# A small token block moved ahead at one turn of the work, and a batch's attention begun one stage earlier

## The chip, the cores and the metric

One core of a Trainium2 chip runs one program. The metric is the device time of one execution in microseconds (us). TensorE (PE) does the matmuls, VectorE (DVE), ScalarE (ACT) and GpSimd (POOL) the elementwise work, SyncE (SP) issues most transfers.

## What is computed

Three layers follow one another, all in float32:

```python
def _attn_ref(q, k, v):                       # 4 batches, 8 heads, 576 rows, 64 wide
    q_s = np.exp(q - q.max(-1)); q_s = q_s / (q_s.sum(-1) + 1e-09)
    k_s = np.exp(k - k.max(2));  k_s = k_s / (k_s.sum(2) + 1e-09)
    kv = np.einsum('bhsd,bhse->bhde', k_s, v)
    return np.einsum('bhsd,bhde->bhse', q_s, kv)

def _moe_ref(x, w_in, w_out):                 # 2304 tokens, 512 -> 2048 -> 512
    h = x @ w_in
    g = np.where(h >= 1, h, np.where(h <= -1, 0.0, (h + 1) ** 2 / 4))
    return g @ w_out

def _moe2_ref(x, domain_probs, w1, w2):       # 4 experts, 512 -> 1024 -> 512
    p = domain_probs / (domain_probs.sum(-1, keepdims=True) + 1e-09)
    for e in range(E):
        out += p[:, e:e + 1] * (np.maximum(x @ w1[e], 0.0) @ w2[e])
    return out
```

The second layer is called layer one below, the third the experts.

## The kernel before, in words

The 2304 tokens are five blocks: 0, 1, 2 and 4 of 512 tokens, 3 of 256. They are worked in two passes (`PASSES`): the first takes blocks 1 and 0 through layer one and then through all four experts, the second blocks 2 and 4 as a pair, with block 3 as its `rest`. Attention of batches 0 and 1 runs at the start of the program, that of batches 2 and 3 beside the first pass; each batch is four units, a unit being two heads.

A float32 product is made of three matmuls on split operands, a high and a low part of each (`products`, lines 1257 to 1261): the `x` tiles hold tokens, the `w` tiles weights, the `gate` tiles hidden values. The hidden layer's products ("ups") go into the PSUM tiles `bank` and `late_bank`; the products of the second matrix ("downs") go into `out_bank`. For a pair of blocks the ups are Strassen's seven products on quarter matrices (`strassen`, line 1449): sums of quarters of the tokens, called B11, T1, B21, T2, T3, T4 and B22, are made once per stage by `prepare` (line 1285), on DVE and POOL, and split into high and low by `split` (a cast on ACT or DVE, line 512 or 514, and a subtraction on DVE or POOL, line 517). Block 3's ups are plain products (`plain_rest`, line 1427). In the experts of the second pass the pair's downs are seven products too (`second_pairs`, line 1770), block 3's are plain (`group_downs`, line 1703).

The work is a list of groups of four chunks of hidden columns (`groups`). In the second pass each quarter or half of a weight matrix stands three times in the list, for blocks 2, 4, 3 in this order. The downs are issued in the order of this list. A group's ups can run ahead of its downs.

Nobody writes the order of instructions by hand. The program is built by a planner (`Order`): tasks are Python generators that ask for an engine and a duration, and of the tasks that can go on the planner takes the one with the earliest due step, with an allowance per kind of task. The order it finds is then fixed in each engine's queue. Steps count the chunks of the list, 0 to 239; the first pass's experts begin at step 32, the second pass at 96, its experts at 144.

What the change touches:

- Where layer one of the second pass ends and the experts begin ("the second turn"): the last downs of layer one are evicted into `acc` by `finish_first` (line 1888, DVE), `prepare` forms the seven sums out of `acc2` and `acc4` (blocks 2 and 4), and only then can the experts' first Strassen products run. Block 3's operand is split after all of the pair's operands are (`yield operands_in`).
- The same place of the first pass ("the first turn"), with blocks 1 and 0.
- Attention of batches 2 and 3: `load_units` (line 919) holds the first unit back until the event `calm`, which is set in `ups` when the second group of the first pass's experts begins, and the units' due steps are `to_experts + 10 + 5 * n`. A unit's PE instructions are transposes (lines 1108, 1112, 1206) and float32 matmuls (1138, 1216, two records for each), its DVE work is in lines 1105, 1110, 1171, 1190 and 517. When the last unit is done, `end_attention` gives its room to ten more gate tiles and one more PSUM bank to the ups.

Of the kernel before, what the change touches and what calls it, by code (L numbers as in the profile page):

```python
# [206 lines left out]
def attention_moe_kernel(  # L207
# [17 lines left out]
    KC = DM // P  # L225
# [37 lines left out]
    GATE_DUE = 1  # L263
    groups = []
    for pair, rest in PASSES:
        bs = [bi for bi in (*pair, rest) if bi is not None]
        for ws in (first, *experts):
# [5 lines left out]
            for i in range(0, len(ws), nj):  # L273
                groups += [(bi, ws[i:i + nj]) for bi in bs]
# [319 lines left out]
    part_in = {(ws[0], u): Event() for ws in jobs if len(ws) > 1 for u in range(4)}  # L594
    second_in = {(ws[0], u): Event() for ws in jobs if is_paired(ws[0]) for u in range(4)}
# [53 lines left out]
    def convert_weights():  # L649
        for ws in jobs:  # L650
# [20 lines left out]
            if is_paired(w):  # L671
# [6 lines left out]
                slot_of[w, 1] = us  # L678
                order.add(load_sums(w, 1, us[1:3], second_in), "load", due + 1)
# [593 lines left out]
    xop = {}  # L1273
    xop_in = {(i, kind, x, c): Event()
# [10 lines left out]
    def prepare(i, kind):  # L1285
# [63 lines left out]

        for k, x in enumerate(USE):  # L1350
            xop[i, kind, x] = ((yield xfree), (yield xfree))
            if not ts:
# [10 lines left out]
        if rest is not None:  # L1363
            xop[i, kind, "rest"] = ((yield xfree), (yield xfree))
            for c in range(KC):
                for event in come(rest, c):
                    yield event
            h, l = xop[i, kind, "rest"]
            yield operands_in[i, kind]
            t = yield from split(h, l, acc[rest], 1024)  # L1370
            rest_in[i, kind].set(t)
            used[rest].set(t)
# [9 lines left out]
    def ups():  # L1382
        for s, (g, j) in enumerate(steps):
# [3 lines left out]
            if w[0] == "b" or is_kept(w):  # L1387
                i, kind = w[3], w[0]
                pair, rest = PASSES[i]
                if bi == pair[0] and j % 2 == 0:  # L1390

                    ahead = 4 if kind == "a" and g == order_of[bi, kind][-1] else 0
# [8 lines left out]
                    if rest is not None:  # L1401
                        for k in range(2):
                            yield from plain_rest(i, g + 2, j + k)
# [4 lines left out]
            yield s  # L1408
            bank = yield ups_banks
# [13 lines left out]
            if s == last_a[bi]:  # L1423
                for x in xparts[bi]:
                    xfree.put(x, t)

# [22 lines left out]
    def strassen(i, g, j):  # L1449
# [7 lines left out]
        kind = w0[0]  # L1457
        at_end = j + 2 == len(ws) and g == order_of[bi, kind][-1]
# [512 lines left out]
```

## Time and profile before

| | |
|---|---|
| median of 3 runs | 1248.21 us (1247.08 to 1250.82) |
| the profiled execution | 1249.59 us |
| its span, first to last instruction | 1247.8 us |
| PE busy | 1221.9 us, 98% |
| DVE, POOL, ACT busy | 876.0, 683.9, 493.2 us |
| mean granted TensorE clock | 0.995 of full speed |

The engines' times overlap. A matmul's record is longer than its place in the queue: the next one starts before it ends, so the step from one start to the next is what a matmul costs PE, and idle time is what lies beyond the record's end.

### The profile page before, as it was taken

Reading aid. Unit: us, or ns where it says so; the run is one execution under the profiler, and the core shown is the slowest. Engines: PE = TensorE matmul, PEld = TensorE weight load, DVE = VectorE, ACT = ScalarE, POOL = GpSimd, SP = SyncE. Lnnn points to the kernel's source line nnn. Section 1 sums busy time; section 2 is a strip of 40 time slices with the busy share of each in tenths; the row PEclk is TensorE's granted clock in tenths of the full one; section 3 lists DMA queues with packets and bytes.
Section 4 is the critical chain, followed back from the end, with each engine's and each line's share of the span. In section 5 each row is a group of like instructions: output and inputs, shape, how many; then the busy total and the mean of one; then the engine's idle time right before and its main releaser. Section 6 shows DMA issues by size and latency. Waiting matters only on the chain.

```text
span 1247.8 us, 16455 instructions
## 1 busy us (share of the span) xinstructions
PE 1221.9 (98%) x5876; PEld 1007.1 (81%) x5876; DVE 876.0 (70%) x1318; ACT 493.2 (40%) x884; POOL 683.9 (55%) x595
## 2 busy tenths in 40 slices
PE   9999999999999999999999999999999999999996
PEld 8877778767787788888888888778888888888885
DVE  4866783699877877776733554578778777787786
ACT  4655654343443542232373354434223232232321
POOL 4453555444654565543785654343665675576653
PEclk9999999999999999999999999999999999999999
DMA  9863554225656453342553131504344244433313
GB/s 266 240 221 134 205 192 164 68 89 188 209 188 175 148 174 147 136 169 93 162 185 101 35 101 51 186 17 153 118 151 137 102 136 142 145 119 118 114 40 85
DMA packets 101170, 174.68 MB, mean 140 GB/s; under 512 B 25568, under 2 KB 59360, under 8 KB 101088
## 3 DMA queue, kind: packets, MB, share of 16 engines
q1 hardware_dynamic: 100288, 172.31, 42.1%
q10 hardware_dynamic: 800, 1.31, 0.4%
q8 instruction: 47, 0.77, 0.2%
q14 instruction: 35, 0.29, 0.1%
HBM read 118.53 MB, written 55.07 MB: 139 GB/s over the span
## 4 chain that ended last, share of the span: by engine, by line
PE 88%; DVE 7%; DMA 2%; ACT 1%; issue 1%; POOL 1%; SPq 0%; ACTq 0%; DVEq 0%; POOLq 0%
PE out_bank L1259 14%; PE out_bank L1260 14%; PE out_bank L1261 14%; PE bank L1259 7%; PE bank L1260 7%; PE bank L1261 7%; PE late_bank L1259 6%; PE late_bank L1260 6%; PE late_bank L1261 6%; PE bank L1254 2%; PE third L993 1%; DVE single L841 1%; PE late_bank L1138 1%; PE late_bank L1216 1%; DVE w L517 0%
## 5 line engine op out<-in xcount | busy, mean ns | idle before, releaser
L1259 PE MATMUL bank<-x,w 128*128 128x512 f32 (+1 forms) x490 | 185.5, 379 | 4.2 <-DVE cv L1689 2.2
L1260 PE MATMUL bank<-x,w 128*128 128x512 f32 (+1 forms) x490 | 182.5, 372 | 2.9 <-DVE x L517 2.7
L1261 PE MATMUL bank<-x,w 128*128 128x512 f32 (+1 forms) x490 | 182.0, 371 | 0.0
L517 POOL TENSOR_TENSOR w<-words,w 128x512 fp32r<-128x512 f32 (+2 forms) x87 | 116.9, 1355 | 110.7 <-ACT w L512 73.0
L1259 PE MATMUL late_bank<-x,w 128*128 128x512 f32 (+1 forms) x390 | 142.8, 366 | 1.4 <-POOL w L517 1.1
L1260 PE MATMUL late_bank<-x,w 128*128 128x512 f32 (+1 forms) x390 | 141.6, 363 | 0.0
L1261 PE MATMUL late_bank<-x,w 128*128 128x512 f32 (+1 forms) x390 | 141.4, 362 | 0.0
L1821 DVE TENSOR_TENSOR acc<-out_bank,acc 128x512 f32<-128x512 f32 x182 | 121.0, 687 | 24.9 <-PE out_bank L1261 24.6
L517 POOL TENSOR_TENSOR gate<-cv,gate 128x512 fp32r<-128x512 f32 (+1 forms) x59 | 76.1, 1298 | 93.2 <-ACT gate L512 91.8
L1259 PEld LDWEIGHTS bank<-x,w 128*128 128x128 f32 x490 | 92.4, 188 | 23.2 <-DVE cv L1689 3.0
L1260 PEld LDWEIGHTS bank<-x,w 128*128 128x128 f32 x490 | 92.5, 189 | 19.8 <-DVE x L517 4.3
L517 POOL TENSOR_TENSOR gate_late<-cv,gate_late 128x512 fp32r<-128x512 f32 (+1 forms) x57 | 72.1, 1272 | 60.6 <-ACT gate_late L512 60.3
L1261 PEld LDWEIGHTS bank<-x,w 128*128 128x128 f32 x490 | 92.3, 188 | 16.0
L1259 PE MATMUL out_bank<-w,gate 128*128 128x512 f32 x216 | 89.7, 415 | 0.3 <-DVE acc L1902 0.3
L1259 PE MATMUL out_bank<-gate,w 128*128 128x512 f32 (+1 forms) x224 | 85.5, 381 | 2.3 <-DVE acc L1888 2.3
L1259 PEld LDWEIGHTS late_bank<-x,w 128*128 128x128 f32 x390 | 73.7, 189 | 15.3 <-POOL w L517 1.5
L1260 PE MATMUL out_bank<-gate,w 128*128 128x512 f32 (+1 forms) x224 | 85.5, 382 | 0.0
L1261 PE MATMUL out_bank<-w,gate 128*128 128x512 f32 x216 | 85.4, 395 | 0.0
L1260 PE MATMUL out_bank<-w,gate 128*128 128x512 f32 x216 | 85.3, 395 | 0.0
L1261 PE MATMUL out_bank<-gate,w 128*128 128x512 f32 (+1 forms) x224 | 85.1, 380 | 0.0
L1260 PEld LDWEIGHTS late_bank<-x,w 128*128 128x128 f32 x390 | 73.8, 189 | 12.6 <-DVE x L517 0.4
L1261 PEld LDWEIGHTS late_bank<-x,w 128*128 128x128 f32 x390 | 73.8, 189 | 11.6
(320 smaller groups left out, 2919.4 us busy)
## 6 DMA issues: line engine op xcount, KB each, us to landing
words<-in_moe_w_dram SPq DMA_DIRECT2D x64, 512.0 KB, 4.5
sums<-w SPq DMA_DIRECT2D x64, 512.0 KB, 3.2
w<-sums SPq DMA_DIRECT2D x64, 512.0 KB, 4.3
kept<-w SPq DMA_DIRECT2D x32, 512.0 KB, 4.8
w<-kept SPq DMA_DIRECT2D x32, 512.0 KB, 4.9
words<-in_moe_w_in_dram SPq DMA_DIRECT2D x16, 512.0 KB, 3.8
words<-in_moe_w_out_dram SPq DMA_DIRECT2D x16, 512.0 KB, 5.2
wide<-in_q_dram SPq DMA_DIRECT2D x22, 160.0 KB, 3.2
```

What stands on the lines that cost most here:

```text
L517: (nc.vector if engine == DVE else nc.gpsimd).tensor_tensor(**kw)
L841: nc.vector.scalar_tensor_tensor(out=bits, in0=low, scalar=29, in1=bits, op0=ALU.logical_shift_right, op1=ALU.bitwise_or)
L993: nc.tensor.matmul(bank[:, :P].rearrange("p (h d) -> p h d", h=2), ek[:n, c], vt[:n, :, c], start=(c == 1), stop=(c == 0),)
L1138: nc.tensor.matmul(bank[:, :N], ek[:, c, :], vt_buf[:, c * N:(c + 1) * N], start=(c == 0), stop=(c == NC - 1),)
L1216: nc.tensor.matmul(bank[:, :hi - lo], bd, qt_buf[:, lo:hi], start=True, stop=True)
L1254: nc.tensor.matmul(bank[:, :P], ident, ident, start=True, stop=True)
L1259: nc.tensor.matmul(ps, al, bh, start=first, stop=False, **kw)
L1260: nc.tensor.matmul(ps, ah, bl, start=False, stop=False, **kw)
L1261: nc.tensor.matmul(ps, ah, bh, start=False, stop=last, **kw)
L1821: nc.vector.tensor_tensor(out=dst, in0=p, in1=dst, op=ALU.add)
```

## The change

The list of groups is altered at two places: the last quarter of layer one of the second pass goes in the order 2, 3, 4, and the first half of expert 0 in the order 3, 2, 4. At the first Strassen product of the experts, block 3's four plain products for that half are issued between the first and the second of the seven (`AT_TURN`). For them block 3's operand of the experts is split first and waits no longer for the pair's. The last Strassen group of layer one may start 6 steps ahead instead of 4 (`AHEAD_A`). The first weights of the second pass's experts are no longer held back until the pair's operands are there (`NO_WAIT`). Attention of batches 2 and 3 is due ten steps earlier, at the experts' first step, and is let go at step 28, under layer one of the first pass (`CALM`). The rest is bookkeeping for the planner (`xop_at`, `second_slots`, `beside`).

```diff
+    AT_TURN = 2
+    CALM = 28
+    LATE_AT = 0
+    LATE_BY = 5
+    NO_WAIT = 2
+    AHEAD_A = 6
...
-                groups += [(bi, ws[i:i + nj]) for bi in bs]
+                turned = bs
+                if rest is not None:
+                    if ws is first and i + nj == len(ws):
+                        turned = [pair[0], rest, pair[1]]
+                    elif ws is experts[0] and i == 0:
+                        turned = [rest, *pair]
+                groups += [(bi, ws[i:i + nj]) for bi in turned]
...
-        if step_of[w][0] > min(step_of[x][0] for x in chunks if (x[0], x[3]) == (w[0], w[3])):
+        if step_of[w][0] > min(step_of[x][0] for x in chunks if (x[0], x[3]) == (w[0], w[3])) + (NO_WAIT if w[0] == "b" and w[3] else 0):
             yield operands_in[w[3], w[0]]
...
-        att_due[b, hp] = s0 + LAG * hp if b < NOW else to_experts + 10 + 5 * ((b - NOW) * NP + hp)
+        att_due[b, hp] = s0 + LAG * hp if b < NOW else to_experts + LATE_AT + LATE_BY * ((b - NOW) * NP + hp)
...
+        if rest is not None and kind == "b":
+            xop[i, kind, "rest"] = ((yield xfree), (yield xfree))
+            order.add(rest_operand(i, kind, come, used), "ffn", due - 1)
...
-                    ahead = 4 if kind == "a" and g == order_of[bi, kind][-1] else 0
+                    ahead = AHEAD_A if kind == "a" and g == order_of[bi, kind][-1] else 0
...
-                    if g > order_of[0, "b"][0] and calm.time is None:
+                    if s >= CALM and calm.time is None:
                         calm.set(order.running.time)
...
-                    yield from strassen(i, g, j)
-                    if rest is not None:
-                        for k in range(2):
-                            yield from plain_rest(i, g + 2, j + k)
+                    of_rest = None if rest is None else beside(g, rest)
+                    turn = AT_TURN if rest is not None and of_rest < g else 0
+                    yield from strassen(i, g, j, 0 if j else turn)
+                    for k in ([j // 2] if not turn else [] if j else range(turn, len(ws) // 2)):
+                        if rest is not None:
+                            yield from rest_pair(i, of_rest, 2 * k)
...
+            if s == CALM and calm.time is None:
+                calm.set(order.running.time)
...
         if begins:
+            for k in range(turn):
+                yield from rest_pair(i, beside(g, PASSES[i][1]), 2 * k)
             p5 = yield from fifth()
```

**PE, the first turn.** The last downs of layer one and the experts' first products. `late_bank0` with `wide` or `ident` is attention's, `x12` and `x14` are T1 and B21, `x8` is T2. Before:

```order
L1261 MATMUL out_bank3_557<-gate2_1664,w2_94 128x512
L1259 MATMUL bank1_123<-x12_83,w5_97 128x512
...
L1259 MATMUL late_bank1_966<-x14_85,w4_96 128x512
...
L1261 MATMUL late_bank1_966<-x14_85,w4_96 128x512
L1259 MATMUL bank0_122<-x8_79,w5_97 128x512
```

After:

```order
L1275 MATMUL out_bank3_557<-gate2_1664,w2_94 128x512
L1230 MATMUL late_bank0_965<-wide0_136,kvbd00_141 128x256
L1273 MATMUL bank1_123<-x12_83,w5_97 128x512
...
L1230 MATMUL late_bank0_965<-wide0_136,kvbd00_141 128x320
...
L1273 MATMUL late_bank1_966<-x14_85,w4_96 128x512
...
L1152 MATMUL late_bank0_965<-wide4_140,wide3_139 128x130 x5
...
L1273 MATMUL bank0_122<-x8_79,w5_97 128x512
```

Three pieces of attention, of the first two units, now stand between the last down and the first product on T2; before, the first unit's matmuls came only after the turn.

**PE, the second turn.** `gate1` in the first piece is block 3's, `x2` is B11 and `x14` T1; in the second piece `gate2` is block 4's, `x14` is B11, `x2` block 3's operand, `x8` T1. Before:

```order
L1261 MATMUL out_bank3_557<-gate1_1663,w4_96 128x256
L1259 MATMUL bank0_122<-x2_73,w5_97 128x512
...
L1259 MATMUL late_bank0_965<-x14_85,w6_98 128x512
```

After:

```order
L1275 MATMUL out_bank3_557<-gate2_1664,w13_105 128x512
L1273 MATMUL late_bank0_965<-x14_85,w5_97 128x512
...
L1273 MATMUL bank0_122<-x2_73,w5_97 128x256
...
L1273 MATMUL out_bank0_554<-w3_95,gate_late8_3402 128x512
...
L1273 MATMUL bank1_123<-x8_79,w2_94 128x512
```

Before, the 48 matmuls of block 3's last downs (256 columns) stood between block 4's last down and the first product, and T1 came right behind it. Now block 4's downs come last, and between the first product and T1 stand block 3's four ups (12 matmuls of 256 columns each) and four products of its downs (12 matmuls of 512 columns).

**DVE, the second turn.** From the eviction of block 4's sums into `acc4` on. Before:

```order
L1888 TENSOR_TENSOR acc4_91<-out_bank3_557,acc4_91 128x512
L517 TENSOR_TENSOR acc2_89<-acc4_91,cv4_110 128x512
L517 TENSOR_TENSOR x15_86<-cv4_110,x14_85 128x512
L517 TENSOR_TENSOR x15_86<-cv3_109,x14_85 128x512
L517 TENSOR_TENSOR acc2_89<-acc4_91,cv3_109 128x512
L517 TENSOR_TENSOR x5_76<-acc2_89,x4_75 128x512
L1888 TENSOR_TENSOR acc3_90<-out_bank0_554,acc3_90 128x256
```

After:

```order
L1931 TENSOR_TENSOR acc4_91<-out_bank3_557,acc4_91 128x512
L529 TENSOR_TENSOR acc2_89<-acc4_91,cv4_110 128x512
L529 TENSOR_TENSOR x9_80<-cv4_110,x8_79 128x512
L529 TENSOR_TENSOR x9_80<-cv7_113,x8_79 128x512
L529 TENSOR_TENSOR acc2_89<-acc4_91,cv7_113 128x512
L1696 SCALAR_TENSOR_TENSOR gate_late8_3402<-bank0_122,gate_late8_3402 128x256
L1696 SCALAR_TENSOR_TENSOR gate_late9_3403<-bank1_123,gate_late9_3403 128x256
L529 TENSOR_TENSOR x11_82<-acc2_89,x10_81 128x512
```

Block 3's evictions into `acc3` and the split of its operand now stand ahead of block 4's evictions; in the chain of the pair's operands stand instead the four second halves of block 3's hidden values (line 1696).

## Rows read from the trace of the kernel before

**Rows 1.** PE's waits in the whole span: total us, times, longest.

```profile
PE bank L1260 <- DVE x L517: 2.7, 3, 1.6
PE out_bank L1259 <- DVE acc L1888: 2.3, 2, 1.9
```

**Rows 2.** Windows by stage; PEclk is the granted clock.

```profile
core 0: us, PE busy (x) PEld busy (x) DVE busy (x) ACT busy (x) POOL busy (x), PEclk, DMA share, GB/s
196.00:243.00 47.00, 47.00 (x206) 38.34 (x205) 20.50 (x28) 21.77 (x35) 29.83 (x26) 1.00 0.36 123
243.00:262.00 19.00, 17.14 (x68) 12.00 (x67) 17.21 (x26) 8.87 (x17) 6.17 (x4) 1.00 0.00 1
262.00:300.00 38.00, 36.91 (x159) 29.32 (x160) 35.43 (x56) 12.77 (x22) 19.20 (x22) 1.00 0.52 173
300.00:430.00 130.00, 127.23 (x588) 101.66 (x587) 103.75 (x172) 54.00 (x110) 72.44 (x81) 1.00 0.56 180
...
795.00:806.00 11.00, 8.69 (x38) 6.80 (x37) 7.33 (x17) 4.26 (x9) 2.57 (x2) 0.84 0.56 192
...
835.00:843.00 8.00, 6.37 (x20) 4.23 (x19) 7.30 (x10) 3.28 (x5) 5.76 (x4) 0.79 0.00 0
```

**Rows 3.** PE in time, 795 to 806: start, duration, operation, idle before, releaser.

```profile
797.84 0.40 PE L1261 MATMUL out_bank<-gate,w 128*128 128x512 f32 x1
800.12 0.51 PE L1259 MATMUL out_bank<-gate,w 128*128 128x512 f32 x1 [1.88 <-DVE acc L1888]
...
801.63 0.58 PE L1259 MATMUL out_bank<-gate,w 128*128 128x512 f32 x1
...
805.28 0.40 PE L1259 MATMUL out_bank<-gate_late,w 128*128 128x512 f32 x1
805.51 0.39 PE L1260 MATMUL out_bank<-gate_late,w 128*128 128x512 f32 x1
```

**Rows 4.** PE in time, 834 to 843.

```profile
836.83 0.40 PE L1259 MATMUL bank<-x,w 128*128 128x512 f32 x1
838.80 0.50 PE L1260 MATMUL bank<-x,w 128*128 128x512 f32 x1 [1.57 <-DVE x L517]
...
842.82 0.39 PE L1261 MATMUL out_bank<-gate_late,w 128*128 128x512 f32 x1
```

**Rows 5.** DVE in time, 821 to 842.

```profile
821.35 2.79 DVE L1888 TENSOR_TENSOR acc<-out_bank,acc 128x512 f32<-128x512 f32 x4 [6.48 <-PE out_bank L1261]
...
825.21 2.39 DVE L517 TENSOR_TENSOR x<-cv,x 128x512 fp32r<-128x512 f32 x2
827.52 0.68 DVE L517 TENSOR_TENSOR acc<-acc,cv 128x512 f32<-128x512 f32 x1
...
838.06 2.98 DVE L517 TENSOR_TENSOR x<-acc,x 128x512 fp32r<-128x512 f32 x3
```

**Rows 6.** POOL in time, 820 to 842.

```profile
822.18 2.56 POOL L517 TENSOR_TENSOR cv<-acc,acc 128x512 f32<-128x512 f32 x2 [9.19 <-DVE acc L1888]
824.70 1.75 POOL L517 TENSOR_TENSOR acc<-acc 128x512 f32<-128x512 f32 x1
```

**Rows 7.** PE in time, 247.5 to 264.

```profile
261.25 0.40 PE L1261 MATMUL bank<-x,w 128*128 128x512 f32 x1
262.76 0.50 PE L1259 MATMUL late_bank<-x,w 128*128 128x512 f32 x1 [1.11 <-POOL w L517]
```

**Rows 8.** PE in time, 312 to 318 and 446.5 to 451.5.

```profile
315.59 0.59 PE L1216 MATMUL late_bank<-wide,kvbd 128*128 128x256 f32 x2
315.83 0.58 PE L1259 MATMUL late_bank<-x,w 128*128 128x512 f32 x1
...
447.92 1.28 PE L1138 MATMUL late_bank<-wide,wide 128*128 128x130 f32 x10
448.95 0.48 PE L1259 MATMUL out_bank<-w,gate 128*128 128x512 f32 x1
```

**Rows 9.** Groups of instructions by line, attention's on DVE.

```profile
L1171 DVE TENSOR_REDUCE mq<-wide 128x10 f32<-128x640 f32 x8 | 6.5, 811 | 0.0
```

More of the change, by code (lines that the diff above doesn't have):

```diff
@@ L678, in convert_weights @@
                 slot_of[w, 1] = us
+                second_slots[w].set(order.running.time)
                 order.add(load_sums(w, 1, us[1:3], second_in), "load", due + 1)
@@ L1273, in attention_moe_kernel @@
     xop = {}
+    xop_at = {(i, kind, x): Event() for i in range(len(PASSES)) for kind in "ab" for x in USE}
     xop_in = {(i, kind, x, c): Event()
@@ L1362, in prepare, with rest_operand @@
         order.add(give_temps(), "ffn", due - 1)
-        if rest is not None:
+        if rest is not None and kind == "a":
             xop[i, kind, "rest"] = ((yield xfree), (yield xfree))
[L1365 to L1368, printed above, removed]
+            yield from rest_operand(i, kind, come, used)
+    def rest_operand(i, kind, come, used):
+        rest = PASSES[i][1]
+        for c in range(KC):
+            for event in come(rest, c):
+                yield event
+        h, l = xop[i, kind, "rest"]
+        if kind == "a":
             yield operands_in[i, kind]
-            t = yield from split(h, l, acc[rest], 1024)
-            rest_in[i, kind].set(t)
-            used[rest].set(t)
+        t = yield from split(h, l, acc[rest], 1024)
+        rest_in[i, kind].set(t)
+        used[rest].set(t)
     def prepare_all():
@@ L1425, in ups, with beside, rest_pair @@
                     xfree.put(x, t)
+    def beside(g, bi):
+        return next(x for x in range(max(g - 2, 0), g + 3) if groups[x] == (bi, groups[g][1]))
+    def rest_pair(i, g, j):
+        for k in range(2):
+            yield from plain_rest(i, g, j + k)
     def plain_rest(i, g, j):
@@ L1447, in plain_rest, with strassen @@
         order.add(closed(g, j, bank[:, :n], n, lambda t: ups_banks.put(bank, t)), "ffn")
[L1449 removed]
+    def strassen(i, g, j, turn=0):
         w0 = used(g, j)
@@ L1457, in strassen @@
         kind = w0[0]
+        other = beside(g, PASSES[i][0][1])
         at_end = j + 2 == len(ws) and g == order_of[bi, kind][-1]
@@ L1465, in product @@
             wh, wl = of_part(u, k)
+            yield xop_at[i, kind, b]
             h, l = xop[i, kind, b]
@@ L1509, in of_both @@
             if pairs:
-                yield from weighted(g + 1, j + 1, h, n, None, h)
+                yield from weighted(other, j + 1, h, n, None, h)
             else:
-                yield from closed(g + 1, j + 1, h, n, lambda t: temps.put(h, t), False)
+                yield from closed(other, j + 1, h, n, lambda t: temps.put(h, t), False)
         def of_first(bank):
@@ L1524, in of_second @@
             temps.put(tile["s"], t)
-            yield from close(g + 1, j, bank, n, lambda t: ups_banks.put(bank, t))
+            yield from close(other, j, bank, n, lambda t: ups_banks.put(bank, t))
         def first():
@@ L1802, in second_pairs @@
             units.put(x, t)
+        for x in (w, used(g, j + 1)):
+            if groups[steps[step_of[x][1]][0]][0] in PASSES[1][0]:
+                units.put(slot_of.pop(x), t)
     def add_pair(a, c, p, first, last, seen, give):
```

4 lines of the change are left out of this document (3 added, 1 removed).

## The prediction, made before the changed kernel ran

> **What bounds the kernel now.** I read the windows by stage first. From 300 to 430 us PE is busy 127.23 of 130 us, and the stages I do not list are fuller still [rows 2]. So no engine's speed is at stake: PE does the same 5408 queue rows before and after the change, and what can be gained is PE's waiting, and the time in which PE works at half its clock. The list of PE's waits says who makes it wait: the seven sums of the tokens (line 517, 2.7 us in 3 waits) and the evictions of layer one (line 1888, 2.3 us in 2 waits) lead it [rows 1]. The windows say where: at the two turns. From 243 to 262 PE is idle for 1.86 of 19 us, with DVE busy 17.21; from 795 to 806 for 2.31 of 11 us and from 835 to 843 for 1.63 of 8 us, and in these two alone the granted clock is below 1.00 (0.84 and 0.79) [rows 2].
>
> **What the second turn costs, read from starts.** At full clock one 512-column matmul follows the other after 0.23 us (805.28 to 805.51) [rows 3]. The reader is to see three things there. From 797.84 to 800.12 one step took 2.28 us, 2.05 too long, since DVE was late with an eviction; with the wait of 0.43 us in front of it (the eviction waits sum to 2.3, the longest is 1.9) [rows 1] that is 2.5. From 801.63 to 805.28 nine steps took 3.65 us where 2.07 would do [rows 3]: PE waits for nothing, its granted clock has fallen, to the lower of its two levels (1.2 GHz of 2.4), after the idle time; 1.6 lost. From 836.83 to 838.80 one step took 1.97 us, 1.74 too long, waiting for the last sum, T4; and from 838.80 to 842.82 ten steps took 4.02 us for 2.3, again 1.7 lost to the clock [rows 4]. Together 2.5 + 1.6 + 1.7 + 1.7 = 7.5 us.
>
> **The change part by part.**
>
> *Block 3 as cover at the second turn.* Why T4 is late: from block 4's last evictions, DVE does four at 0.70 us (2.79 from 821.35), POOL the two differences T1 (1.28 each, from 822.18), then the chain goes on through T2, T3 and T4 on DVE, ACT and POOL, and its last subtractions stand on DVE at 838.06 [rows 5, 6]: some 15.5 us after block 4's last down was issued. Before, PE had as cover in this time block 3's last downs (48 matmuls of 256 columns) and the first five of the seven products; it ran out 1.7 us too early. Now block 3's downs are out of the chain and its work for the experts is in it: 48 matmuls of 256 columns, the same as went, and 12 of 512, 12 x 0.23 = 2.8 us more [rows 3]. Block 3's part of the chain stays as long: four evictions of 256 columns stood in it, four second halves of hidden values of that width stand in it now. T1 is due 2.8 us later after block 4's last down than before, and T4 as well: 2.8 covers 1.7, with 1.1 to spare. The T4 wait goes, and with it its half-clock stretch: 3.4 us.
>
> What is late next: right behind T4's product PE wants the sum of three products out of DVE (line 1507), two operations of 0.69 us after the third product has ended, where one product of 1.4 us lies between. I put 0.5 us there. Then block 3's downs of the same half need their weights, whose split stands on DVE behind nine operations of the first sums: 0.6 us.
>
> *Block 3 in front of block 4 in layer one's last quarter.* The eviction wait at 800.12 came because block 3's four evictions stood on DVE behind the hidden values of the last Strassen group, and only one product of each sum (12 matmuls of 256) covered them. Now 24 more of these matmuls stand there, 24 x 0.12 = 2.9 us (a step of 256 columns at half the time of 512), against waits of 2.3. I keep 0.3 us of it, and as one DVE operation may go slow beside POOL (below) 0.6 more. Six steps ahead instead of four only lets the ups start earlier; cover that is already there, nothing.
>
> So of 7.5 us stay 0.5 + 0.6 + 0.3 + 0.6 = 2.0; **5.5 gained**. Bounds: 7.5, if none of the four appears, and 0.
>
> *Attention earlier, at the first turn.* The work of a unit is the same, so no price changes; what counts is what it now lies beside. The order puts three pieces of it behind the last down and ahead of T2's product. From the rows a piece on line 1138 advances PE by 1.03 us (447.92 to 448.95), one on line 1216 by 0.24 and, by the longer step after it (0.58 us record), some 0.2 more [rows 8]: 1.03 + 2 x 0.45 = 1.9 us. PE's waits there (1.86 us up to 262, and 1.11 at 262.76 for a weight that POOL splits) [rows 2, 7] are longer than that, so attention would lie in idle time and save up to 1.9 where it stood before, at 300 to 430 us. Against it stand two reductions of 0.81 us each that the new order puts into the DVE queue of this chain [rows 9], ACT's copies of attention's results, and a subtraction of attention's on POOL ahead of the weight. Between a gain of 1.9 and a loss of 1.6 I take **1.0 gained**, nearer to the gain, since the first reduction is queued behind the eviction of the third of four sums, where DVE waits for PE anyway. A unit also issues its loads (keys, queries, values) on SP some 60 us earlier, past the stores of weight sums; from 196 to 243 the transfers take 0.36 of the DMA engines [rows 2], so I cost them at nothing; the cover is PE's own queue of ready ups, and if it were gone a load of a few us would show.
>
> *Attention earlier, in the experts.* From 300 to 430 PE idles 2.77 us, DVE is busy 103.75 of 130 [rows 2]. The units keep their spacing of five steps, so the stretch moves to some 250 to 380 us and is as full. I count no change; bounds, all of the 2.77 gone or as much again. The room that the last unit frees comes some 50 us earlier, where PE did not wait: nothing. Weights no longer held back, the planner's events: nothing, PE did not wait for them.
>
> **The sum.** The profiled execution took 1249.59 us with a span of 1247.8: 1249.59 - 5.5 - 1.0 = 1243.1. The median of the runs is 1.4 lower than this execution, so against the median 1248.21 - 6.5 = **1241.7**.
>
> **A rule against it.** DVE's two subtractions from 825.21 took 2.39 us while POOL's at 824.70 took 1.75 instead of 1.28; the one at 827.52, with POOL idle, took 0.68 [rows 5, 6]. So the two slow each other down, and by a factor. By the Trainium skill (GPSIMD Engine Reference, Key points) POOL shares its interfaces to SBUF with VectorE, with contention for VectorE instructions that have two SBUF inputs. By that rule every such subtraction of the chain can go slow, as the trace shows for these two; without it, those would be chance.
>
> **The rivals.** *The chain gets slower by as much as its cover grew.* In the new order five DVE operations on SBUF alone stand beside POOL's three (T1's two differences, then T3's and B22's splits). At 1.2 instead of 0.68 us each, five cost 2.6 us more; T4 is then late by 2.6 - 1.1 = 1.5 us, with the half clock's 1.7 behind it: 3.2 given back, 1244.9. For it: the row at 825.21. Against: before, the chain had the same pairs and its T4 time already holds them. The sentence on the rule stands beside this case; chance 0.15.
>
> *Attention's DVE work delays the first turn.* All of the 1.6 us is lost instead of 1.0 won, 1244.3, or with one wait more of the kind seen in 300 to 430, 1246. Chance 0.11.
>
> *DVE becomes the bound from 243 to 300, slower than before.* DVE is busy 17.21 of 19 and 35.43 of 38 us there [rows 2], 4.4 us free. A unit costs DVE at least 0.81 x 2 for its reductions and about as much twice over for its subtractions and maxima, say 4.7 us [rows 9]. If the two and a half units that now come before 300 put all of it behind 243 rather than into the 26.5 free us of 196 to 243 [rows 2], PE loses 12 - 4.4 = 7.6, and half clock behind two such waits 3.3: 1241.7 + 1.0 + 10.9 = 1253.6. It decides from 5 us of delay that find no cover. Against: the units are let go at step 28, and DVE is free for more than half of that stretch. Chance 0.06.
>
> *More is gained than I count*: nothing stays at the second turn and the middle's waits go as well: 1248.21 - 7.5 - 1.9 - 2.8 = 1236. Chance 0.08.
>
> **How the numbers follow.** My case has 0.60, from 1239 to 1243.5. A measurement of this kernel can tell a change of 0.3%, 3.7 us, from none: the bounds are 1244.5 and 1251.9. Faster: my case, the last rival, and 0.07 of the first two, 0.75. Same: the rest of these, 0.19. Slower: 0.06. The range leaves out the slow rival and the far half of the last: 1237.5 to 1246.0.
>
> **What would show it.** In the changed profile: no wait on `x` at line 517 over 0.5 us and no wait on `acc` of layer one's evictions over 0.5 us at the second turn, and the granted clock at 1.00 in the windows around it. A wait on `cv` from the sums (line 1544 there) of about 0.5 us right behind the turn. At the first turn, waits of 1 to 2 us in sum instead of 3. From 250 to 400 us about as much idle time on PE as from 300 to 430 before. Wrong it is if T4 is still waited for, if the clock falls at another place, or if PE's waits between 196 and 300 grow over 4 us.

## The result, and the profile after

The changed kernel took 1237.84 us (median of 5, 1237.36 to 1238.42), the kernel before 1249.38 us beside it (median of 5, 1247.08 to 1250.82). The ratio is 0.991, with a 95% interval from 0.9895 to 0.9924: faster by 11.5 us, 0.9%. The forecast was 6.5 us. The profiled execution took 1237.97 us, 11.6 less than the one shown of before; its span is 1236.2 us, PE is busy 1216.8 us of it (98%), DVE 873.5, POOL 687.4, ACT 495.8, and the mean granted clock is 0.999.

PE's waits after, over the whole span (total us, times, longest). The two rows that led the list before, for the sums of the tokens and for layer one's evictions [rows 1], have no successor among these; what is left at the second turn is one wait for a weight:

```profile
PE bank L1273 <- DVE cv L1728: 1.6, 1, 1.6
...
PE out_bank L1274 <- DVE w L529: 1.2, 1, 1.2
...
PE late_bank L1122 <- DVE mk L1119: 0.7, 1, 0.7
PE bank L1273 <- DVE cv L1544: 0.6, 1, 0.6
```

The windows by stage, the columns as in [rows 2]:

```profile
196.00:243.00 47.00, 46.33 (x205) 37.66 (x205) 23.07 (x38) 25.12 (x41) 32.62 (x31) 1.00 0.39 124
243.00:262.00 19.00, 18.84 (x94) 15.07 (x93) 16.66 (x26) 7.71 (x16) 8.16 (x7) 1.00 0.49 153
262.00:300.00 38.00, 36.50 (x159) 27.87 (x158) 32.02 (x53) 15.88 (x32) 22.89 (x23) 1.00 0.39 134
300.00:430.00 130.00, 129.81 (x598) 103.97 (x598) 100.77 (x168) 57.42 (x121) 71.85 (x82) 1.00 0.56 181
780.00:806.00 26.00, 26.00 (x155) 23.12 (x154) 18.55 (x32) 12.45 (x22) 7.73 (x6) 1.00 0.64 218
830.00:860.00 30.00, 28.59 (x122) 22.24 (x121) 23.64 (x35) 12.45 (x22) 10.13 (x8) 1.00 0.21 70
```

From 780 to 806 us PE has no idle time at all, and the clock stays at 1.00 through the second turn. But the stretch from 300 to 430 us, of which I had expected nothing, went from 2.77 us of idle time [rows 2] to 0.19.

To see how much of the gain lies where, one needs two products that are the same in all orders. PE waits for `cv` at about 180 us in every kernel, before any order differs, and again at about 617 us, when attention is over and the second turn is still far. Before and after (start, duration, idle before, releaser):

```profile
179.94 0.50 PE L1259 MATMUL bank<-x,w 128*128 128x512 f32 x1 [1.60 <-DVE cv L1689]
...
620.80 0.50 PE L1259 MATMUL bank<-x,w 128*128 128x512 f32 x1 [0.28 <-DVE cv L1507]
```

```profile
180.72 0.50 PE L1273 MATMUL bank<-x,w 128*128 128x512 f32 x1 [1.60 <-DVE cv L1728]
...
616.80 0.50 PE L1273 MATMUL late_bank<-x,w 128*128 128x512 f32 x1 [0.28 <-DVE cv L1544]
```

From the first to the second is **stretch A**: 440.86 us before, 436.08 after, 4.8 less. From the second to the end of the span is **stretch B**: 1247.8 - 620.80 = 627.0 before, 1236.2 - 616.80 = 619.4 after, 7.6 less. The start is 0.8 us longer; it differs from one execution to the next, 179.36 to 182.04 us in the fourteen traces. So attention (A) was worth 4.8 where I had put 1.0 in sum, and the second turn (B) 7.6 where I had put 5.5.

### The profile page after: what moved, and what is told of

Its sections match the earlier page's. It is cut to its first block, busy times and chain, and to the rows that moved or that the text cites. A ratio compares the mean times of both kernels' runs of the same rounds, so it can differ in the third digit from the quotient of the medians.

```text
span 1236.2 us, 16431 instructions
## 1 busy us (share of the span) xinstructions
PE 1216.8 (98%) x5876; PEld 1005.3 (81%) x5876; DVE 873.5 (71%) x1310; ACT 495.8 (40%) x890; POOL 687.4 (56%) x598
## 4 chain that ended last, share of the span: by engine, by line
PE 88%; DVE 7%; ACT 2%; issue 1%; DMA 1%; SPq 1%; POOL 0%; ACTq 0%; DVEq 0%
PE out_bank L1273 14%; PE out_bank L1274 14%; PE out_bank L1275 14%; PE bank L1273 7%; PE bank L1275 7%; PE bank L1274 7%; PE late_bank L1273 6%; PE late_bank L1274 6%; PE late_bank L1275 6%; PE bank L1268 1%; PE third L1007 1%; DVE single L855 1%; PE late_bank L1152 1%; PE late_bank L1230 1%; DMA acc<-in_v_dram 1%
## 5 line engine op out<-in xcount | busy, mean ns | idle before, releaser
L529 POOL TENSOR_TENSOR w<-words,w 128x512 fp32r<-128x512 f32 (+2 forms) x87 | 113.3, 1316 | 115.4 <-ACT w L524 81.3
L1273 PEld LDWEIGHTS bank<-x,w 128*128 128x128 f32 x498 | 94.0, 189 | 20.6 <-DVE cv L1728 2.0
L1274 PEld LDWEIGHTS bank<-x,w 128*128 128x128 f32 x498 | 93.9, 189 | 15.9 <-DVE x L529 0.5
L1275 PEld LDWEIGHTS bank<-x,w 128*128 128x128 f32 x498 | 93.8, 188 | 15.6
L529 POOL TENSOR_TENSOR gate<-cv,gate 128x512 fp32r<-128x512 f32 (+1 forms) x56 | 71.3, 1279 | 62.8 <-ACT gate L524 61.1
L1273 PEld LDWEIGHTS late_bank<-x,w 128*128 128x128 f32 x382 | 72.1, 189 | 15.7 <-DVE gate L1696 1.0
L524 ACT CAST w<-words 128x512 fp32r<-128x512 f32 (+2 forms) x110 | 66.0, 616 | 43.3 <-PE out_bank L1275 30.1
L1275 PEld LDWEIGHTS late_bank<-x,w 128*128 128x128 f32 x382 | 72.0, 188 | 12.1
L1274 PEld LDWEIGHTS late_bank<-x,w 128*128 128x128 f32 x382 | 72.1, 189 | 11.7
L1274 PE MATMUL out_bank<-gate_late,w 128*128 128x512 f32 (+1 forms) x216 | 81.3, 376 | 0.0
L1273 PE MATMUL out_bank<-gate_late,w 128*128 128x512 f32 (+1 forms) x216 | 81.1, 375 | 0.0
```

The source lines that it names most:

```text
L524: nc.scalar.copy(out=dst, in_=src)
L529: (nc.vector if engine == DVE else nc.gpsimd).tensor_tensor(**kw)
L1273: nc.tensor.matmul(ps, al, bh, start=first, stop=False, **kw)
L1274: nc.tensor.matmul(ps, ah, bl, start=False, stop=False, **kw)
L1275: nc.tensor.matmul(ps, ah, bh, start=False, stop=last, **kw)
```

## The experiments

All twelve kernels compute the whole reference; they differ in order alone. Their numbers together, each ratio against runs of the kernel before on the same chip:

| kernel | median us | ratio, 95% interval | A us | B us |
|---|---|---|---|---|
| before | 1249.38 | | 440.86 | 627.0 |
| after | 1237.84 | 0.991 (0.9895 to 0.9924) | 436.08 | 619.4 |
| att_only | 1242.68 | 0.9941 (0.9924 to 0.9958) | 435.87 | 625.0 |
| turn_only | 1243.28 | 0.9953 (0.9936 to 0.997) | 441.30 | 619.8 |
| lead_only | 1244.75 | 0.9968 (0.9956 to 0.9981) | 440.85 | 621.8 |
| att_lead | 1239.43 | 0.9923 (0.9909 to 0.9936) | 435.77 | 621.6 |
| ahead4 | 1241.58 | 0.9936 (0.9919 to 0.9952) | 435.72 | 623.3 |
| no_cover | 1244.15 | 0.9956 (0.994 to 0.9972) | 435.89 | 627.4 |
| old_quarter | 1238.53 | 0.9913 (0.9899 to 0.9926) | 435.77 | 619.2 |
| one_pair | 1237.92 | 0.9909 (0.9896 to 0.9923) | 435.70 | 620.0 |
| late5 | 1238.12 | 0.9909 (0.9896 to 0.9923) | 436.05 | 619.7 |
| late10_by6 | 1242.58 | 0.9954 (0.9941 to 0.9967) | 440.50 | 619.8 |
| late13 | 1242.26 | 0.9948 (0.9936 to 0.996) | 439.68 | 619.8 |
| early5 | 1248.02 | 0.9995 (0.9986 to 1.0004) | 445.27 | 620.7 |

A and B are of the one profiled execution. The changed kernel and four with its rules for the second turn and attention elsewhere agree in B to 0.4 us (619.4 to 619.8; `early5`, the fifth, is 0.9 above), and the seven kernels with its attention agree in A to 0.4 us (435.70 to 436.08), so differences of some 1.5 us and more in these columns can be read.

**Each half alone.** In `att_only` the kernel before gets the earlier attention and nothing else:

```diff
-        att_due[b, hp] = s0 + LAG * hp if b < NOW else to_experts + 10 + 5 * ((b - NOW) * NP + hp)
+        att_due[b, hp] = s0 + LAG * hp if b < NOW else to_experts + 5 * ((b - NOW) * NP + hp)
...
-                    if g > order_of[0, "b"][0] and calm.time is None:
+                    if s >= 28 and calm.time is None:
...
+            if s == 28 and calm.time is None:
+                calm.set(order.running.time)
```

> The kernel before with one part of the change: the third batch's attention begins ten steps earlier (its due times without the 10, its release at step 28). The turns, the order of the products and the conditions of loads stay as before. The prediction counted 1.0 us gained at the first turn and nothing in the experts. By that, 1.0 us under the kernel before, and the idle time of PE between 262 and 640 us about as before. The rival drawn from the two traces: the middle itself gains, because the attention's maxima and reductions no longer fall among the reads that PE waits for; then 4 to 5 us under the kernel before, with the waits that stood at 374 and 377 us (0.84 and 1.04 us) gone. At the second turn both expect the idle time as before, with half the granted clock behind it.

In `turn_only` the changed kernel has attention where it was:

```diff
-    CALM = 28
-    LATE_AT = 0
+    CALM = 40
+    LATE_AT = 10
```

> The changed kernel with the attention where it was before (begun at step 40, ten steps later due). What is left is the order of the products at the second turn and the conditions that go with it. The prediction's terms give 5.5 us under the kernel before. The account from the two traces (second turn about 6.5, the middle about 5 by the attention) gives 6 to 7 us under the kernel before, that is 4.5 to 5.5 above the changed kernel. If instead the middle gained through the other parts, this run comes within 2 us of the changed kernel. Granted clock 1.0 at the second turn by both.

Measured: `att_only` is 6.7 us under the kernel before, `turn_only` 6.1 us. The two add up to 12.8, a little more than the whole, 11.5. By the stretches they are apart: A of `att_only` is that of the changed kernel, B of `turn_only` is within 0.4 of it. So the forecast of no gain in the experts falls. `att_only` gained 2.0 more in B than it should; its trace has such waits at the second turn too (4.8 us of idle time from 780 to 860 us, 4.3 before) but only one fall of the clock, of which below.

**What the second turn owes to the lead.** `ahead4` takes the lead of layer one's last Strassen block back from 6 steps to 4 in the changed kernel; `lead_only` gives the kernel before a lead of 6 and nothing else:

```diff
-    AHEAD_A = 6
+    AHEAD_A = 4
```

> The changed kernel with the lead of layer one's last Strassen block put back from 6 steps to 4. The prediction counted that lead as nothing. By that, within 0.3 us of the changed kernel. Rival: with the lead back at 4 fewer of the small block's products lie behind the last Strassen sums, and the evictions are waited for again as before: idle time of about 1 to 2.5 us on layer one's evictions at the turn, and with it perhaps the fall of the granted clock (1.6 us): 1 to 4 us above the changed kernel.

```diff
-                    ahead = 4 if kind == "a" and g == order_of[bi, kind][-1] else 0
+                    ahead = 6 if kind == "a" and g == order_of[bi, kind][-1] else 0
```

> The kernel before with one number of the change: the last Strassen block of layer one may start 6 steps ahead instead of 4. Three groups of the small block's downs (36 matmuls of 256 columns) then stand behind the last Strassen sums, where one stood. The prediction's term for this lead is 0. Theory from the run that put the lead back to 4 (3.7 us lost): the lead alone is worth about as much here, the eviction wait at 795 to 806 us and the half clock behind it go, 3 to 4.5 us under the kernel before; the wait on T4 at 835 to 843 us stays, with or without its half clock. Rival: without the new order of the last quarter the lead does nothing; within 1 us of the kernel before.

Measured: `ahead4` is 3.7 us above the changed kernel, `lead_only` 4.25 us under the kernel before. The wait and the fall of the clock come back and go together with this one number. PE in time in `ahead4`, at the end of layer one; the first row is the last matmul of the one 256-column group (12 matmuls) that is left behind the block's ups:

```profile
791.40 0.28 PE L1275 MATMUL out_bank<-gate_late,w 128*128 128x256 f32 x1
793.75 0.50 PE L1273 MATMUL out_bank<-gate,w 128*128 128x512 f32 x1 [2.07 <-DVE acc L1931]
...
795.50 0.63 PE L1273 MATMUL out_bank<-gate,w 128*128 128x512 f32 x1
795.92 0.63 PE L1274 MATMUL out_bank<-gate,w 128*128 128x512 f32 x1
```

Steps of 0.42 us instead of 0.23 show the half clock behind the wait. With a lead of 6, the ups end earlier and two more groups of downs of 256 columns (24 matmuls) stand behind them; DVE then has time for the hidden values that are queued ahead of block 3's evictions, and 780 to 806 us is full.

**Whether the new order of layer one's last quarter matters.** I had given those 24 matmuls to the new order. `old_quarter` puts it back:

```diff
-                    if ws is first and i + nj == len(ws):
-                        turned = [pair[0], rest, pair[1]]
-                    elif ws is experts[0] and i == 0:
+                    if ws is experts[0] and i == 0:
```

> The changed kernel with the order of blocks in layer one's last quarter put back to 2, 4, 3 and all else kept: lead of 6 steps, block 3 ahead in the experts. The prediction put the eviction wait (2.3 us and the clock behind it) down to the new order; by that, 2.5 to 4 us above the changed kernel with an idle time at 790 to 797 us. Rival: the lead did it, the eviction wait stays away; but block 3's four evictions and the split of its operand then stand late, right ahead of its experts' ups, so a wait of 1.5 to 4 us comes at the first product on block 3's tokens, at about 821 us, while T4 has 5.8 us more cover. The two are told apart by the place of the idle time. If neither comes, the new order of the quarter is worth nothing and this run is within 1 us of the changed kernel.

Measured: 1238.53 us, the changed kernel's time within its interval. The eviction wait stays away, so the lead did it, not the order: the wait is there with a lead of 4 in either order (the kernel before, `ahead4`), and gone with a lead of 6 in either (`lead_only`, the changed kernel). The other wait of the text does come, at block 3's first products, 1.3 us long:

```profile
823.12 0.39 PE L1272 MATMUL bank<-x,w 128*128 128x256 f32 x1 [1.32 <-DVE x L527]
```

In exchange the wait for a weight (1.2 us) is no longer in PE's list: one wait took the place of another, and the new order of the quarter is worth nothing that can be measured.

**What block 3 ahead in the experts is worth.** `no_cover` keeps the new order but issues block 3's ups behind the whole first Strassen set:

```diff
         if begins:
-            for k in range(turn):
-                yield from rest_pair(i, beside(g, PASSES[i][1]), 2 * k)
...
+        for k in range(turn):
+            yield from rest_pair(i, beside(g, PASSES[i][1]), 2 * k)
```

> The changed kernel with all four pairs of the small block's up products of the experts behind the whole first Strassen set, as they were before; layer one's last quarter keeps its new order. Without them ahead, the first product that needs a sum of the second pass stands 1.4 us behind the small block's last down product and the one that waited before (T4) 6.9 us behind it. Theory of the prediction, that the cover before T4 is what removes the wait: the wait comes back as 1.7 us or more, and with it the half clock: 4 to 9 us above the changed kernel. Rival, that the new order in layer one alone brings the sums early enough: 2 us or less above the changed kernel, with the clock at 1.0.

`one_pair` issues half of them ahead:

```diff
-    AT_TURN = 2
+    AT_TURN = 1
```

> The changed kernel with one of block 3's two pairs of ups at the turn instead of both (AT_TURN 1): 24 matmuls of 256 columns less stand ahead of T1's and T4's products, 2.9 us. In the changed kernel T4's operand is ready 1.8 us before its product starts (833.65 against 835.45 us). By the cover theory up to 1.1 us of wait on T4 comes back, less what the chain on DVE gains by two second halves of hidden values fewer in it (0.8 us); and the wait of 1.2 us for the weight of block 3's second downs (split on DVE) moves or goes, since that weight is wanted later. Sum: between 1.2 us under and 0.5 us above the changed kernel; 3 us or more above it if the clock falls behind a new wait.

`att_lead` has the earlier attention and the lead, and block 3 as it was before in both places (the edits of `att_only` and `lead_only` together).

> The kernel before with two parts of the change, the earlier attention and the lead of 6 steps; block 3 stays behind blocks 2 and 4 at the second turn in layer one and in the experts. If the parts add, 6.7 and 4.3 us, this run is 11 us under the kernel before, at about 1238.2, and within 1 us of the changed kernel: then moving block 3 ahead, the part by which the change is named, brings nothing over the lead. It will still show the wait on T4 (1.6 us in the run with the lead alone, without a fall of the clock). Rival: the clock falls behind that wait as in the kernel before, 1.6 us, and block 3's move is worth that and the wait: 1241 to 1242.

Measured: `no_cover` is 6.3 us above the changed kernel, as the cover theory had it. PE in time in `no_cover`: both halves of T1, then T3, then T4 are waited for.

```profile
822.38 0.50 PE L1274 MATMUL bank<-x,w 128*128 128x512 f32 x1 [1.85 <-DVE x L529]
...
824.06 0.68 PE L1274 MATMUL bank<-x,w 128*128 128x512 f32 x1 [0.72 <-DVE x L529]
...
831.11 0.50 PE L1274 MATMUL late_bank<-x,w 128*128 128x512 f32 x1 [1.75 <-DVE x L529]
...
835.57 0.50 PE L1274 MATMUL late_bank<-x,w 128*128 128x512 f32 x1 [2.10 <-DVE x L529]
```

But that is against an order which block 3's downs have left. Against the old order, where those downs were the cover, the move is worth little: `att_lead`, without it, took 1239.43 us, 1.6 above the changed kernel, and the intervals of the two ratios overlap. B is 2.2 longer in `att_lead` than after, and 2.0 longer in `lead_only` than in `turn_only`; I take **about 2 us** from these two pairs, of which PE's idle time and longer steps from 812 to 860 us show 1.3 and 1.6. The pairs differ in the weights no longer held back (`NO_WAIT`) as well, and no run took that part alone. The wait on T4 is there as foretold (1.5 us), with the clock at 1.00. `one_pair` is level with the changed kernel: 1.70 and 0.64 us of waits on T4 and the sum after it, and no wait for the weight.

```profile
833.10 0.50 PE L1274 MATMUL late_bank<-x,w 128*128 128x512 f32 x1 [1.70 <-DVE x L529]
835.39 0.50 PE L1274 MATMUL late_bank<-x,w 128*128 128x512 f32 x1 [0.64 <-DVE x L529]
```

There I had expected up to 1.1 us on T4; it was 0.6 more, and the fall of the clock that would have cost did not come.

**Why attention gains: place or neighbours.** Four more kernels move the units of attention, all with the new second turn:

| | let go at step | due later by | steps between units | units begun before the first turn |
|---|---|---|---|---|
| early5 | 22 | -5 | 5 | 4 |
| after | 28 | 0 | 5 | 2 |
| late5 | 28 | 5 | 5 | 2 |
| turn_only | 40 | 10 | 5 | 0 |
| late10_by6 | 40 | 10 | 6 | 0 |
| late13 | 40 | 13 | 5 | 0 |

> The changed kernel with the third and fourth batch's attention due five steps later, half way to where it was before; let go at step 28 as in the changed kernel. If the middle gains because attention lies earlier, where DVE has room, half of it goes: about 2 to 3 us above the changed kernel. If it gains because units in the kernel before happened to put a reduction or maxima on DVE just ahead of a product that PE waited for, there is no rule in it: waits of 0.3 to 1 us at other places, anything from 0 to 5 us above the changed kernel, and the first turn, where the waits of the changed kernel sum to 2.3 us, as before or changed by up to 1 us. The second turn stays as in the changed kernel by both.

> The changed kernel with attention let go at step 40 and due ten steps later, as before, but with six steps between its units instead of five, so that each piece lies beside other products of the experts than before. Theory one, that late attention costs by where it lies (no unit under layer one, none of its pieces in the idle time of the first turn, all of them beside the experts): about as the run with attention as before, 4 to 6 us above the changed kernel, with 6 to 7 us of waits on PE between 196 and 640 us. Theory two, that in the kernel before two or three units happened to put reductions and maxima on DVE ahead of a product that PE waited for: with other neighbours the waits of 0.8 and 1.0 us and some of those of 0.3 to 0.6 us go or come anew, 1 to 4 us above the changed kernel, and the first turn as before (1.9 us of idle time from 243 to 262).

> The changed kernel with attention let go at step 40 and due 13 steps later than in it, three later than before, five steps between units as before. A second draw of neighbours for the same question. Theory one (place): 4 to 6 us above the changed kernel, or a little more. Theory two (neighbours): anything from 1 to 6 us above it, and different from the run with attention as before by the waits in the stretch from 300 to 430 us.

> The changed kernel with attention let go at step 22 and due five steps earlier still, so that three or four units lie under layer one of the first pass and the fifth at the first turn. Theory one (place): one more unit under layer one, where DVE has room: 0.5 to 2 us under the changed kernel, with fewer waits from 262 to 430 us. Theory two (neighbours): no rule; within 2 us of the changed kernel on either side. If layer one's own evictions are then waited for, PE's idle time from 150 to 243 us, 0.7 us in the changed kernel, grows to 2 us or more and the run is slower than the changed kernel.

Measured, in A: with no unit ahead of the turn 441.30, 440.50 and 439.68, with two 436.08 and 436.05, with four 445.27. The neighbours matter by up to 1.6 us among the late ones, the place by 3.6 to 5.2. `late5` shows it best: its waits lie elsewhere than in the changed kernel (1.2 us at 256 us, 0.7 at 272, 0.8 at 427, by its trace), and the stretch takes the same time to 0.03 us. That it is so near is luck: PE waits 1.0 us longer there and its other steps take 1.0 us less. Half-way due times did not cost half. What the two kernels share is that the first unit's products of keys and values (line 1152) come at 243 to 245 us, at the turn, and that the second unit is begun; of that second unit, `late5` has only the maxima ahead of the turn (242 us). Two orders of the one kind and three of the other are few, but they lie apart by more than twice what the late ones differ among themselves. PE in windows, `late13` and then `late10_by6` (after has 440.92 busy in the long one, before 437.42):

```profile
300.00:430.00 130.00, 128.80 (x588) 1.00 0.56 178
196.00:640.00 444.00, 439.15 (x1960) 1.00 0.47 154
```

```profile
300.00:430.00 130.00, 129.19 (x593) 1.00 0.56 177
196.00:640.00 444.00, 438.62 (x1956) 1.00 0.47 154
```

So idle time from 196 to 640 us is 6.6 us before, 4.9 and 5.4 in these two, and 3.1 after. From `late13` to after that is 1.8 of the 3.6 us by which A differs; the other half is no idle time but steps that are longer than their width asks. All of A can be split so, since its 1933 matmul records are the same in number in every order: idle times over 0.15 us sum to 5.9 us before and 2.4 after, 3.5 of the 4.8 us gained, and the other steps of PE to 1.2 us less. They are not those behind attention's float32 matmuls: the 56 steps right behind one are 7.2 us longer in sum than the usual 0.2275 us each, before, in `late13` and after alike. What lengthens the others is open.

Nor is it the number of units in a stretch, or how busy DVE is. From 300 to 430 us lie the matmuls on line 1138 (1152 in the changed kernel and its variants) of six units before and of five each in `late13`, `late10_by6` and after; DVE is busy 103.75, 102.25, 105.36 and 100.77 us; PE is idle for 2.77, 1.20, 0.81 and 0.19. So the two late kernels lose more than half of the waits in this window with other neighbours, and no unit has left the experts in them. That the earlier place is worth 3.6 to 5.2 us is measured; by what it is, the runs show in part only.

How a neighbour costs can be seen in the kernel before. DVE in time there, and then PE:

```profile
374.04 0.81 DVE L1190 TENSOR_REDUCE sq<-wide 128x10 f32<-128x640 f32 x1
374.77 0.68 DVE L1657 SCALAR_TENSOR_TENSOR gate<-bank,gate 128x512 fp32r<-128x512 f32 x1
...
376.37 1.27 DVE L1105 TENSOR_TENSOR mk<-wide 128x128 f32<-128x128 f32 x1
377.67 1.24 DVE L1105 TENSOR_TENSOR mk<-mk,wide 128x128 f32<-128x128 f32 x1
```

```profile
375.60 0.47 PE L1259 MATMUL bank<-x,w 128*128 128x512 f32 x1 [0.84 <-DVE gate L1657]
...
378.96 0.33 PE L1108 MATMUL late_bank<-ident,mk 128*128 128x128 f32 x1 [1.04 <-DVE mk L1105]
```

A reduction of attention's stands on DVE just ahead of the hidden value for which PE waits 0.84 us; then PE stands still 1.04 us at the next unit's transposes, since its maxima take 1.27 and 1.24 us. `late13` and `late10_by6` lose these two waits and get others, among them 1.1 us at 406 us in the one and 0.7 at 357 in the other.

`early5` fell to the other side: 10 us slower than the changed kernel, level with the kernel before. I had expected it within 2 us, or slower through layer one's evictions. Of the waits of its PE from 196 to 300 us, 4.6 of 8.0 us name attention's own matmuls (lines 1152, 1220, 1230), among them:

```profile
PE late_bank L1230 <- ACT acc L524: 2.1, 2, 1.7
PE bank L1273 <- DVE w L529: 1.6, 2, 1.2
...
PE late_bank L1230 <- ACT wide L524: 0.8, 1, 0.8
PE late_bank L1152 <- DMA wide<-in_v_dram: 0.8, 1, 0.8
```

The units' matmuls stand in PE's queue before their operands are there, and everything behind them waits; the rest are waits of the experts' products for weights, hidden values and sums out of DVE. Together 7.9 us of idle time from 196 to 300 us, against 2.3 after. None of the twelve is faster than the changed kernel beyond the measurement.

## Why the prediction was right, and where it was not

The time lay in the forecast's range, and the direction and the first cause, waits at the turns and the half clock behind them, hold. But it lay only 0.3 us inside, 1237.84 against a low end of 1237.5, and outside the 1239 to 1243.5 of my own case. That the range held is luck in part. Its low end came from a rival and not from the sum, which put 6.5 us where 11.5 were; and the kernel before took 1249.38 us beside it, not the 1248.21 that I had started from, off which the gain of 11.5 would have come to 1236.7. Step by step:

- **The second turn, 5.5 us gained: 7.6 in stretch B.** All of the 7.5 us of waits and half clock are gone but for new waits of 1.17 and 0.15 us, where I had left 2.0. Of the four remainders, the wait for the sum of three products was 0.15 instead of 0.5, those for evictions did not come, and the one for block 3's weight was twice my 0.6. From 780 to 860 us, PE's idle time and what its steps take beyond 0.2275 us (512 columns) and 0.12 (256) sum to 9.2 us before and 2.9 after, so the turn itself gave 6.3: 4.6 up to 812 us, where I had 3.2 (2.5 + 1.6 less 0.9), and 1.7 behind it, where I had 2.3 (3.4 less 1.1). The rest of B is small change at other places that I did not follow up.
- **"Six steps ahead instead of four only lets the ups start earlier; cover that is already there, nothing."** This step failed, though the sum did not show it: its gain stood in the sum under another name, and that was luck. The 24 matmuls of 256 columns that I counted as new cover were counted rightly, but I gave them to the new order of the quarter. They come from the lead: `lead_only` gained 4.25 us with it alone, `old_quarter` lost nothing without the new order.
- **Block 3 as cover, 3.4 us (T4's wait and its half clock).** The wait went, as worked out, but with more to spare. The last half of T4's operand is ready on POOL at 833.65 us (832.36 + 1.29), 2.7 ahead of the matmul that needs it (the one at which PE waited before), where I had 1.1:

```profile
832.36 1.29 POOL L529 TENSOR_TENSOR x<-acc,x 128x512 fp32r<-128x512 f32 x1 [5.95 <-ACT x L524]
```

```profile
836.36 0.39 PE L1274 MATMUL late_bank<-x,w 128*128 128x512 f32 x1
```

The reason is that the chain to T4 was 2.0 us shorter, which I had not counted: from the start of block 4's last down it takes 13.8 us (819.87 to 833.65), before 15.8 (823.02 to 838.80). So the wait went by a shorter chain as well as by more cover. The half clock of 1.7 behind the wait should not have been put down as a sure part of the wait: with the lead alone the same wait of 1.6 us stood without it. Block 3's move is worth about 2 us.

- **The first turn, 1.0 gained.** The waits sank from 2.97 us [rows 2, 7] to 0.16 up to 262 us and 0.63 + 0.44 + 0.19 behind it, 1.4, as foretold; a wait of 0.68 us at the first unit's transposes (234.51 us) was not. Net 0.9 by these rows, and 0.6 by all idle time from 196 to 300 us (2.9 before, 2.3 after), near my 1.0.
- **"The units keep their spacing of five steps, so the stretch moves to some 250 to 380 us and is as full. I count no change"** is the step that cost the forecast most, 3.8 us of stretch A. From 270 to 430 us PE waits 3.0 us before and 0.3 after, though the stretch is about as full, as I had said. From 250 to 400 us it idles 1.85 us, and most of that is the turn's. I had asked what the moved units gain where they go and not what goes from the place they leave. What of the old place made PE wait is seen at single rows (374 to 379 us above); why the new one does so little of it stays open, as said there.
- **"The stages I do not list are fuller still"** is not so of all of them: from 150 to 196 us PE is idle for 2.45 of 46 us before and 2.44 after. The change does not touch that stage.

**The rivals.** Of the chain that slows as its cover grows: DVE's and POOL's rows after, in the chain of the second turn, show the slowing itself.

```profile
820.91 1.24 DVE L529 TENSOR_TENSOR acc<-acc,cv 128x512 f32<-128x512 f32 x1
822.07 1.46 DVE L529 TENSOR_TENSOR x<-cv,x 128x512 fp32r<-128x512 f32 x2
823.45 1.80 DVE L529 TENSOR_TENSOR acc<-acc,cv 128x512 f32<-128x512 f32 x1
...
841.68 1.50 DVE L526 CAST w<-words 128x512 fp32r<-128x512 f32 x1
843.22 1.64 DVE L529 TENSOR_TENSOR w<-words,w 128x512 fp32r<-128x512 f32 x1
```

```profile
823.40 3.01 POOL L529 TENSOR_TENSOR x<-acc,x 128x512 fp32r<-128x512 f32 x2 [1.80 <-ACT x L524]
...
841.20 1.70 POOL L529 TENSOR_TENSOR acc<-cv,acc 128x512 f32<-128x512 f32 x1
842.98 1.33 POOL L529 TENSOR_TENSOR cv<-cv,cv 128x512 f32<-128x512 f32 x1
```

Subtractions of 0.68 us [rows 5] took 1.24 and 1.80 beside POOL's, and the cast and split of block 3's weight 1.50 and 1.64. Casts of this shape on DVE take 0.43 in the median, so the two are 2.0 us over their usual time, more than the wait of 1.17 us for this weight. The contention that the Trainium skill names (GPSIMD Engine Reference, Key points) is there in these rows. But up to T4 it did not grow: the four operations from 820.91 took 4.5 us, the same four before 4.3, 1.23 in this row and 2.39 and 0.68 in [rows 5].

```profile
824.06 1.23 DVE L517 TENSOR_TENSOR acc<-acc,cv 128x512 f32<-128x512 f32 x1
```

That DVE would become the bound did not happen: it is busy 16.66 of 19 and 32.02 of 38 us, less than before. That attention would spoil the first turn did not happen either; `early5` shows that it was five steps of due times and six of release away, more by attention's own operands that come late than by other work on DVE. The rival that more is gained, at 1236, was the nearest to the result: it had both of the things that I had left out, the waits of the middle and more of the turn.

## What to carry to other kernels

When work is moved, price the place that it leaves with the same care as the one that it enters: here 2.7 us of waits went there, for which nothing was forecast. Where an order is written by a planner, say of each block of cover which rule put it there; a lead of two steps did here what a change of the blocks' order was credited with, and only kernels with one of the two tell them apart. And work for a gap must be ready when the gap comes: two units begun ahead of it gained 4.8 us, four cost 4.4.

## What the runs showed of the hardware that I had not expected

The fall of the granted clock does not follow from the length of one wait. It fell behind waits of 1.88 us and 1.57 us in the kernel before [rows 3, 4] and of 2.07 us in `ahead4` and `att_only`. It stayed at 1.00 behind the 1.59 to 1.62 us at 180 us in every kernel, behind 1.67 at 218 us in `early5`, and behind waits on T4 of 1.60 us (`lead_only`), 1.52 (`att_only`) and 1.70 (`one_pair`); in `no_cover` it fell behind 1.85 and 0.72 us close to each other and not behind 1.75 and 2.10 us a little later. PE in windows from 832 to 842 us in `lead_only`, around a wait of 1.60 us, with the granted clock in the third column from the right:

```profile
832.00:842.00 10.00, 7.48 (x31) 1.00 0.00 0
```

What else decides is left open; no run was made for it. It bears on the accounts: part of what `att_only` gained in stretch B is a fall that did not come.
